# Folding the denominators of a sketched attention into its query sketch, in an attention and SwiGLU kernel on one core

## The chip, the core and the metric

The kernel runs on one core of a Trainium2 chip. A core has four engines that compute, each working through its own queue in order: TensorE (PE, matrix multiplies, with its weight loads shown as PEld), VectorE (DVE), ScalarE (ACT) and GpSimd (POOL). A fifth, SyncE (SP), issues transfers. The engines wait for each other through semaphores. Operands lie in SBUF, matmul results in the eight banks of PSUM, from which VectorE and ScalarE take them away. The metric is the device time of one execution in microseconds (us), lower is better.

## The reference

Two blocks follow each other. The first is an attention without a softmax over 4 batches, 4 heads, 1088 positions and 32 channels. Two 8x32 sketch matrices turn each query and key into two vectors of 8, whose outer product is a feature vector of 64:

```python
def phi(x):
    a = np.einsum('rd,bhsd->bhsr', S1, x)
    b = np.einsum('rd,bhsd->bhsr', S2, x)
    return np.einsum('bhsi,bhsj->bhsij', a, b).reshape(*x.shape[:-1], r * r)
q_p, k_p = (phi(q), phi(k))
kv = np.einsum('bhsf,bhsd->bhfd', k_p, v)
z = np.sum(k_p, axis=2)
num = np.einsum('bhsf,bhfd->bhsd', q_p, kv)
den = np.einsum('bhsf,bhf->bhs', q_p, z)[..., None] + 1e-06
```

Its result num / den, heads side by side, is a matrix x of 4352 tokens by 128. The second block is a SwiGLU layer with 1536 hidden channels: g = x @ w_gate, out = (g * sigmoid(g) * (x @ w_val)) @ w_out. Everything is float32.

## The kernel before

**Tiles.** A batch is cut into three blocks of 384, 384 and 320 tokens, so there are 12 blocks. The 1536 hidden channels are 12 chunks of 128. A unit is one block with one chunk. It makes the gate and the value products in PSUM, applies Silu on ScalarE and multiplies, which gives a tile of hidden values. `down` (L936) later multiplies that tile with a chunk of `w_out` and adds it up in the bank "acc". After 12 chunks `store` (L967) transposes the sum on VectorE and sends it out.

**Two kinds of unit.** A plain unit (`unit`, L903) has two float32 matmuls at L911 and one multiply on VectorE (L928). A cut unit (`cut_unit`, L868) replaces a float32 matmul by three in the type float32r, on operands that were split beforehand: weights into w1, wb and wd, tokens into x1, x0 and xd (`cut_weights` L835, `cut_tokens` L850). One (L877) makes a correction, two (L883, L884) add up the main part. ScalarE scales the correction (L889), VectorE joins the two (L892), and the multiply goes to GpSimd (L901). With both=False only the value product is made so and the gate product stays float32 (L879); with both=True both are.

**The order.** It is written out by hand (`manual_schedule`): the order in which Python emits instructions is the order in every engine's queue. Batch 0's attention comes first, in a form of its own, with the loading of the weights beside it. Then comes the head, a loop of 30 units of blocks 0 to 2 (z at L1140) in which downs start at z=17, and a flush of the remaining downs (L1160). The line then goes through the other nine blocks, y from 0 to 107 (L1177), twelve units to a block, each unit followed by a down of an earlier unit. In the line y below 38 is plain, 38 to 47 cuts the value product, 48 to 106 cuts both, and 107 is plain.

**The attention beside it.** The attentions of batches 1 to 3 are one Python generator (`attentions`, L563). The loops call it after a unit and it emits the next few instructions up to a `yield`; `group()` runs it up to a mark "pe". For each batch it transposes keys and queries on VectorE (`turns`), multiplies them with the sketch matrices on TensorE (`key_products` L332, `query_sketches` L320), makes key features on VectorE (L355), sums them on GpSimd (`feature_sums` L525), multiplies features with values and makes the key sums z (`values` L366, L678), and spreads both over the partitions with small transfers (`spread_out`). `query_step` (L706) then makes the denominators on VectorE: the first sketch of every query times z as products of 768 numbers a piece (L719), their sum (L726), times the second sketch (L735), summed, inverted. It scales the first sketch by the inverse, makes query features (L355) and transposes them (L750). `numerators` (L760) multiplies them on TensorE and copies the result to `xT`, the second block's input. For batch 1 numerators come in two parts, tokens of the first third before the line starts.

**PSUM.** Before y=36 units take banks in turn from three; from y=36 on (`oldest`) they take the one of seven that was touched longest ago, save those that are held.

Of the kernel before, what the change touches and what calls it, by code (L numbers as in the profile page):

```python
# [7 lines left out]
FP32 = mybir.dt.float32  # L8
# [11 lines left out]
def kernel(  # L20
# [280 lines left out]
    s12 = const.tile([P, 2 * H, 2, R], FP32, name="s12")  # L301
# [14 lines left out]
    def query_sketches(ps, c0, c1):  # L316

        for c in range(c0, c1):
            for a in range(4):
                nc.tensor.matmul(  # L320
                    ps[32 * a : 32 * a + 32, 64 * (c - c0) : 64 * (c - c0) + 64],
                    qT[:, 4 * c + a, :],
                    s12[:, a : a + H, :, :].rearrange("p h t r -> p (h t r)"),
                    start=True,
                    stop=True,
                )

    def key_products(ps, c0, c1):

        for c in range(c0, c1):  # L330
            for a in (0, 2):
                nc.tensor.matmul(  # L332
                    ps[32 * a : 32 * a + 64, 64 * (c - c0) : 64 * (c - c0) + 64],
                    kT[:, c, a : a + 2, :].rearrange("p a t -> p (a t)"),
                    s12[:, 0:H, :, :].rearrange("p h t r -> p (h t r)"),
                    start=True,
                    stop=True,
                )
# [182 lines left out]
    def feature_sums(phk):  # L521
# [4 lines left out]
        add(s[:], rows[:, 0:4, :], rows[:, 4:8, :])  # L526
        add(s[:, 0:2, :], s[:, 0:2, :], s[:, 2:4, :])
        add(s[:, 0, :], s[:, 0, :], s[:, 1, :])
        add(s[:, 0, :], s[:, 0, :], rows[:, 8, :])
        return s[:, 0, :]  # L530

    def turns(b):

        for c in kpieces:
# [3 lines left out]
            yield  # L538
        for x0, x1 in ((0, 4 * kpieces[0][1]), (4 * kpieces[0][1], 4 * NC)):
# [5 lines left out]
    def sketches(places):  # L545


        for products, i in ((key_products, 2), (query_sketches, 3)):
            for p in places:
                products(p[i], p[0], p[1])  # L550
        both = [
            apool.tile([P, 2, NC * H, R], FP32, tag=n, name=n, bufs=2) for n in ("kabs", "qab")
        ]

        def copy(t, c0, c1, ps):
            nc.scalar.copy(
                t[:, :, H * c0 : H * c1, :],
                ps[:, 0 : 64 * (c1 - c0)].rearrange("p (x t r) -> p t x r", t=2, r=R),
            )

        return both, [(copy, t, p[0], p[1], p[i]) for i, t in ((2, both[0]), (3, both[1])) for p in places]

    def attentions():  # L563
# [3 lines left out]

        yield from turns(1)
        hold("a", "b")
        kp, qp = wide("a"), wide("b")
        for ps, products in ((kp, key_products), (qp, query_sketches)):
            for i, c in enumerate(kpieces):
                products(ps[:, i, :], *c)
        ka = apool.tile([P, NC * H, R], FP32, tag="kas", name="kas")
        qab = apool.tile([P, 2, NC * H, R], FP32, tag="qab", name="qab", bufs=2)
        fac = None, qab  # L580
# [8 lines left out]
        for n, (i, c0, c1) in enumerate(((0, 0, 3), (0, 3, 5), (1, 5, 7), (1, 7, 9))):  # L589
# [3 lines left out]
            if n < 2:  # L593
                q0, q1 = kpieces[n]
                nc.scalar.copy(
                    qab[:, :, H * q0 : H * q1, :], sketch(qp, n).rearrange("p x t r -> p t x r")
                )
            if n == 1:
                release("b")
# [4 lines left out]
        zs = feature_sums(phk)  # L604
        for i, _ in enumerate(turns(2)):
            if i % 2:
                yield
        hold("a", "b")
        kvz = wide("a")
        values(kvz[:, 0, :], phk, zs)  # L610
        kq = wide("b")
        fac2, copies = sketches([
            (0, NC - 1, kq[:, 0], kq[:, 1]),
            (NC - 1, NC, kvz[:, 1, 0 : 2 * F], kvz[:, 1, 2 * F : 4 * F]),
        ])
        spread = spread_out(1, kvz[:, 0, :])
        for _ in range(4):
            yield
            run_copies(copies, 1)
        release("a", "b")  # L620
        step = query_step(1, fac, spread)
        yield from step(0, 3)
        numerators(1, spread, 0, 3)
        yield "first"
        yield from step(3, NC)
        phk = hbuf[:, NH - 6 :, :].rearrange("p s (n h i j) -> p (s n) h i j", h=1, i=R, j=R)
        phk = phk.rearrange("p (c h) o i j -> p c (h o) i j", h=H)
        yield from features(phk, fac2, ())
        zs = feature_sums(phk)
        yield from turns(3)  # L630
        yield "pe"
        numerators(1, spread, 3, NC)
        hold("a", "b")
        kv = bank()
        values(kv, phk, zs)
        kp, qp = wide("a"), wide("b")
        fac3, copies = sketches([(c0, c1, kp[:, i], qp[:, i]) for i, (c0, c1) in enumerate(kpieces)])
        spread = spread_out(2, kv)
        run_copies(copies, 2)
        yield  # L640
        run_copies(copies, 2)
        release("a", "b")
        yield
        yield from features(phk, fac3, ())
        zs = feature_sums(phk)
        yield from query_step(2, fac2, spread)(0, NC)
        yield "pe"
        numerators(2, spread, 0, NC)
        kv = bank()
        values(kv, phk, zs)  # L650
        spread = spread_out(3, kv)
        for _ in range(4):
            yield
        yield from query_step(3, fac3, spread)(0, NC)
        yield "pe"
        numerators(3, spread, 0, NC)
# [7 lines left out]
    def features(phk, fac, copies):  # L664
        kab = fac[0]
        for n, (c0, c1) in enumerate(((0, 3), (3, 5), (5, 7), (7, 9))):
            x = slice(H * c0, H * c1)
            key_features(phk, (kab[:, 0, x, :], kab[:, 1, x, :]), c0, c1)
            if copies:
                run_copies(copies, 1)  # L670
# [12 lines left out]
    def spread_out(b, kv):  # L683
# [3 lines left out]
        spread = apool.tile([P, H, 2, F], FP32, tag="spread", name="spread")  # L687
        nc.scalar.copy(
            spread[:, 0, 0, :].rearrange("p (j i) -> p j i", j=R),
            kv[:, F : 2 * F].rearrange("p (i j) -> p j i", j=R),  # L690
        )
        nc.vector.transpose(
            out=spread[:, 0, 1, :].rearrange("p (g d) -> p g d", g=2),
            in_=kv[:, 0:F].rearrange("p (g f) -> p g f", g=2),
        )
        for s in range(1, H):
            m = P - 32 * s
            nc.sync.dma_start(out=spread[0:m, s, :, :], in_=spread[P - m : P, 0, :, :])
            nc.sync.dma_start(out=spread[m:P, s, :, :], in_=spread[0 : P - m, 0, :, :])
# [6 lines left out]
    def query_step(b, fac, spread):  # L706
        zrep = spread[:, :, 0, :].rearrange("p h (j i) -> p h j i", j=R)
        qab = fac[1]
# [4 lines left out]

        def step(s0, s1):
            thirds = [c for c in fpieces if s0 <= c[0] < s1]
            for c0, c1 in thirds:
                n, x = c1 - c0, slice(H * c0, H * c1)
                f = qab[:, 0, x, :].rearrange("p (c h) i -> p c h i", h=H)
                nc.vector.tensor_tensor(  # L719
                    out=phq[:, c0:c1, :, :, :],  # L720
                    in0=zrep.unsqueeze(1).to_broadcast([P, n, H, R, R]),
                    in1=f.unsqueeze(3).to_broadcast([P, n, H, R, R]),
                    op=ALU.mult,
                )
                yield
                nc.vector.tensor_reduce(  # L726
                    out=dot[:, x, :],
                    in_=phq[:, c0:c1, :, :, :].rearrange("p c h j i -> p (c h) j i"),
                    axis=AX.X,
                    op=ALU.add,  # L730
                )
                yield
            x = slice(H * s0, H * s1)
            w = H * (s1 - s0)
            nc.vector.tensor_tensor(  # L735
                out=dot[:, x, :], in0=dot[:, x, :], in1=qab[:, 1, x, :], op=ALU.mult
            )
            nc.vector.tensor_reduce(out=den[:, x], in_=dot[:, x, :], axis=AX.X, op=ALU.add)
            nc.vector.tensor_scalar_add(den[:, x], den[:, x], 1e-6)
            nc.vector.reciprocal(den[:, x], den[:, x])  # L740
            nc.vector.tensor_tensor(
                out=qab[:, 0, x, :], in0=qab[:, 0, x, :],
                in1=den[:, x].unsqueeze(2).to_broadcast([P, w, R]), op=ALU.mult,
            )
            yield
            for c0, c1 in thirds:
                x = slice(H * c0, H * c1)
                key_features(phq, (qab[:, 0, x, :], qab[:, 1, x, :]), c0, c1)
                yield
                nc.vector.transpose(  # L750
                    out=phT[:, :, :, c0:c1, :].rearrange("p h g c t -> p c (h g) t"),
                    in_=phq[:, c0:c1, :, :, :].rearrange(
                        "p c h (g i) j -> p c (h g) (i j)", g=2
                    ),
                )
                yield

        return step

    def numerators(b, spread, s0, s1):  # L760
        kvr = spread[:, :, 1, :].rearrange("p h (g d) -> p h g d", g=2)
        phT = turned[b]
        num = wide("a"), wide("b")
        for g in range(2):
            for s in range(H):
                for a in range(4):
                    r = slice(32 * a, 32 * a + 32)
                    h = (a + s) % 4
                    n = min(s1, (NX - a + 3) // 4) - s0
# [3 lines left out]
                        phT[r, s, g, s0 : s0 + n, :],  # L773
# [472 lines left out]
```

## Time and profile before

| what | value |
|---|---|
| time, median of 3 runs | 292.65 us (292.53 to 292.82) |
| span of the profiled execution | 290.6 us |
| PE busy | 284.5 us (98%) |
| DVE busy | 200.7 us (69%) |
| ACT busy | 154.5 us (53%) |
| POOL busy | 130.1 us (45%) |
| units begin after the head, y=0 | 92.41 us |
| unit y=38, first cut of the value product | 169.06 us |
| unit y=48, first cut of both | 185.21 us |

Busy shares are averages over stages; the stages can be told apart by the source lines of the matmuls. Matmuls are pipelined and their recorded ends are modelled, so TensorE's pace is read from the starts of successive matmuls.

### The profile page before, as it was taken

To read this page: it belongs to the slowest core of one execution; us is meant where nothing else is said; L and a number is where in the kernel's file an instruction comes from. 1 tells how busy PE (TensorE), PEld (TensorE's weight loads), DVE (VectorE), ACT (ScalarE), POOL (GpSimd) and SP (SyncE) were. 2 spreads that over 40 slices of the span, in tenths; PEclk is the share of its full clock that TensorE was granted. 3 is DMA by queue.
4 is the path that set the end of the run, shared out by engine and by line. 5 is a ranking of instruction groups with operands and counts; after the bars stand their busy time and mean duration, and the time that the engine had idled before them with its cause. 6 is when DMAs were issued, how large, how long until landed. Compare 5 with 4: busy or idle time off the path is not lost.

```text
span 290.6 us, 6170 instructions
## 1 busy us (share of the span) xinstructions
PE 284.5 (98%) x2307; PEld 204.6 (70%) x2307; DVE 200.7 (69%) x400; ACT 154.5 (53%) x369; POOL 130.1 (45%) x144
## 2 busy tenths in 40 slices
PE   8899999999999999999999999999999999999995
PEld 7545566667666555755667677778788988888985
DVE  3997988875542997188893369997567675676651
ACT  3567565431301432353242365578688888888860
POOL 3215322138000308039741039676466676576650
PEclk9999999999999999999999999999999999999999
DMA  7564292315411100140010020001001010020101
GB/s 199 153 211 111 61 314 72 103 55 162 115 20 26 17 0 2 34 104 0 0 28 3 2 50 0 2 0 27 2 1 28 2 23 0 0 32 0 24 2 27
DMA packets 26142, 14.63 MB, mean 50 GB/s; under 512 B 18688, under 2 KB 24192, under 8 KB 26112
## 3 DMA queue, kind: packets, MB, share of 16 engines
q1 hardware_dynamic: 25456, 14.13, 19.1%
q8 instruction: 18, 0.29, 0.4%
q10 hardware_dynamic: 656, 0.10, 0.2%
q14 instruction: 12, 0.10, 0.1%
HBM read 11.41 MB, written 2.23 MB: 47 GB/s over the span
## 4 chain that ended last, share of the span: by engine, by line
PE 91%; DVE 3%; DMA 1%; issue 1%; ACT 1%; POOL 0%; SPq 0%; DVEq 0%
PE PS L911 32%; PE PS L942 28%; PE PS L877 7%; PE PS L883 7%; PE PS L884 7%; PE PS L879 2%; PE PS L770 2%; PE PS L332 2%; PE PS L366 2%; DMA kld<-in_k_dram 1%; PE PS L320 1%; DVE sum L892 1%; PE PS L957 1%; PE PS L475 1%; PE PS L423 1%
## 5 line engine op out<-in xcount | busy, mean ns | idle before, releaser
L942 PE MATMUL PS<-hbuf,wo 128*128 128x384 f32 (+2 forms) x288 | 104.7, 460 | 0.4 <-DVE o L971 0.4
L901 POOL TENSOR_TENSOR hbuf<-sg,sum 128x384 f32<-128x384 f32 (+1 forms) x69 | 69.8, 1015 | 53.6 <-ACT sg L896 31.4
L892 DVE SCALAR_TENSOR_TENSOR sum<-PS,sum 128x384 f32<-128x384 f32 (+1 forms) x128 | 62.7, 527 | 29.4 <-ACT sum L889 27.1
L917 ACT ACTIVATE sg<-PS 128x384 f32<-128x384 f32 (+1 forms) x75 | 35.4, 473 | 68.5 <-PE PS L911 66.1
L942 PEld LDWEIGHTS PS<-hbuf,wo 128*128 128x128 f32 x288 | 52.5, 189 | 17.6 <-issue 0.7
L911 PE MATMUL PS<-xT,wg 128*128 128x384 f32 (+1 forms) x150 | 59.1, 476 | 0.0
L911 PE MATMUL PS<-xT,wv 128*128 128x384 f32 (+1 forms) x150 | 58.3, 470 | 0.2 <-DVE wv L270 0.2
L889 ACT ACTIVATE sum<-PS 128x384 f32<-128x384 f32 (+1 forms) x128 | 53.3, 465 | 5.6 <-PE PS L877 5.2
L928 DVE TENSOR_TENSOR hbuf<-sg,PS 128x384 f32<-128x384 f32 (+1 forms) x69 | 36.1, 524 | 28.6 <-PE PS L911 26.8
L911 PEld LDWEIGHTS PS<-xT,wv 128*128 128x128 f32 x150 | 28.3, 190 | 17.9 <-DVE hbuf L928 0.9
L911 PEld LDWEIGHTS PS<-xT,wg 128*128 128x128 f32 x150 | 27.6, 190 | 18.2 <-issue 1.2
L896 ACT ACTIVATE sg<-sum 128x384 f32<-128x384 f32 (+1 forms) x59 | 29.7, 503 | 17.2 <-DVE sum L892 16.5
L877 PE MATMUL PS<-xd,gphq 128*128 128x384 f32 (+1 forms) x59 | 34.6, 587 | 0.0
L883 PE MATMUL PS<-x,w 128*128 128x384 f32 (+1 forms) x69 | 25.4, 368 | 0.0
L877 PE MATMUL PS<-xd,wd 128*128 128x384 f32 (+1 forms) x69 | 24.6, 357 | 0.0
L884 PE MATMUL PS<-x,wb 128*128 128x384 f32 (+1 forms) x69 | 22.6, 328 | 0.0
L883 PE MATMUL PS<-x,graw 128*128 128x384 f32 (+1 forms) x59 | 19.2, 325 | 0.0
L884 PE MATMUL PS<-x,graw 128*128 128x384 f32 (+1 forms) x59 | 19.1, 324 | 0.0
L877 PEld LDWEIGHTS PS<-xd,wd 128*128 128x128 f32 x69 | 13.1, 189 | 6.8
L838 POOL TENSOR_TENSOR low<-wv,w 128x384 f32<-128x384 f32 x4 | 4.7, 1176 | 25.4 <-ACT w L838 25.4
L877 PEld LDWEIGHTS PS<-xd,gphq 128*128 128x128 f32 x59 | 11.1, 189 | 6.4 <-issue 0.4
L525 POOL TENSOR_TENSOR zs<-hbuf 128x1024 f32<-128x1024 f32 x2 | 4.7, 2364 | 21.5 <-PE PS L911 11.6
(129 smaller groups left out, 340.7 us busy)
## 6 DMA issues: line engine op xcount, KB each, us to landing
kld<-in_k_dram SPq DMA_DIRECT2D x4, 544.0 KB, 4.2
vld<-in_v_dram SPq DMA_DIRECT2D x12, 144.0 KB, 4.8
qld<-in_q_dram SPq DMA_DIRECT2D x3, 544.0 KB, 3.8
raw<-in_moe_w_out_dram SPq DMA_DIRECT2D x4, 384.0 KB, 3.7
out_dram<-o SPq DMA_DIRECT2D x28, 48.0 KB, 1.9
raw<-in_moe_w_gate_dram SPq DMA_DIRECT2D x3, 384.0 KB, 3.2
raw<-in_moe_w_val_dram SPq DMA_DIRECT2D x3, 384.0 KB, 3.3
out_dram<-o SPq DMA_DIRECT2D x16, 40.0 KB, 1.7
```

The lines of the kernel that those rows point to most:

```text
L332: nc.tensor.matmul(ps[32 * a : 32 * a + 64, 64 * (c - c0) : 64 * (c - c0) + 64], kT[:, c, a : a + 2, :].rearrange("p a t -> p (a t)"), s12 ...
L877: nc.tensor.matmul(d, wd, xd, start=True, stop=True)
L883: nc.tensor.matmul(p, w1, x1, start=True, stop=False)
L884: nc.tensor.matmul(p, wb, x0, start=False, stop=True)
L889: nc.scalar.activation(s, d, AF.Copy, scale=-1.0 / BETA)
L892: nc.vector.scalar_tensor_tensor(out=s, in0=p, scalar=1.0 + 1.0 / BETA, in1=s, op0=ALU.mult, op1=ALU.add)
L896: nc.scalar.activation(sg, sums[0] if both else g, AF.Silu)
L901: nc.gpsimd.tensor_tensor(out=hj[:, 0:n], in0=sg, in1=sums[-1], op=ALU.mult)
L911: nc.tensor.matmul(o[:, 0:n], w[:, j, :], xT[:, t0 : t0 + n], start=True, stop=True)
L917: nc.scalar.activation(sg[:, 0:n], g[:, 0:n], AF.Silu)
L928: nc.vector.tensor_tensor(out=hj[:, 0:n], in0=sg[:, 0:n], in1=u[:, 0:n], op=ALU.mult)
L942: nc.tensor.matmul(acc[i][:, 0:n], wo[:, j, :], hidden[i, j][:, 0:n], start=(j == 0), stop=(j == NCH - 1),)
```

## The change

The denominators move from VectorE to TensorE. Since the denominator is a sum over i and j of a_i b_j z_ij, and a is the query times the first sketch, the kernel can fold z and the first sketch into a third sketch of 8x32 for each head and batch (`fold`: w_j = sum over i of z_ij S1_i). The query's matmul then gives three vectors of 8 instead of two, and the denominator is the product of the second and third, summed. The products with z and their sums go. The sketch matmul for queries widens from 64 to 96 columns, and it now has to wait for its batch's key sums.

The order is rewritten with it. Key and query turns are separate; batch 1's numerators come in one part; batches 2 and 3 are grouped at y=6, 8, 22, 24 and 40 instead of 12, 36 and 60. The operands of the value product are split during the head, so that all units of the line from y=0 cut the value product, and those from y=22 cut both, instead of from 38 and 48. The subtraction that makes `low` goes from GpSimd to VectorE. The first add of the feature sums, over 4 rows, becomes two of 2 rows, placed between other work. The oldest-bank rule and the hold of "acc" begin at y=0; a down follows its unit by five units instead of two from the line's start.

```diff
-                    ps[32 * a : 32 * a + 32, 64 * (c - c0) : 64 * (c - c0) + 64],
+                    ps[32 * a : 32 * a + 32, 96 * (c - c0) : 96 * (c - c0) + 96],
                     qT[:, 4 * c + a, :],
-                    s12[:, a : a + H, :, :].rearrange("p h t r -> p (h t r)"),
+                    s123[:, a : a + H, :, :].rearrange("p h t r -> p (h t r)"),
...
-        add(s[:], rows[:, 0:4, :], rows[:, 4:8, :])
-        add(s[:, 0:2, :], s[:, 0:2, :], s[:, 2:4, :])
+            lambda: add(s[:, 0:2, :], rows[:, 0:2, :], rows[:, 4:6, :]),
+            lambda: add(s[:, 2:4, :], rows[:, 2:4, :], rows[:, 6:8, :]),
+            lambda: add(s[:, 0:2, :], s[:, 0:2, :], s[:, 2:4, :]),
...
+    def fold(kv):
+        t = apool.tile([P, R, R], FP32, tag="fold", name="fold")
+        w = apool.tile([P, R], FP32, tag="w", name="w")
+        nc.vector.tensor_tensor(
+            out=t[:], in0=kv[:, F : 2 * F].rearrange("p (i j) -> p i j", j=R),
+            in1=sq[:, 0, :, :], op=ALU.mult,
+        )
+        nc.vector.tensor_reduce(
+            out=w[:], in_=t[:].rearrange("p i j -> p j i"), axis=AX.X, op=ALU.add
+        )
+        nc.vector.tensor_tensor(
+            out=s123[:, :, 2, :],
+            in0=w[:].unsqueeze(1).to_broadcast([P, 2 * H, R]),
+            in1=own2[:].unsqueeze(2).to_broadcast([P, 2 * H, R]),
+            op=ALU.mult,
+        )
...
-                nc.vector.tensor_tensor(
-                    out=phq[:, c0:c1, :, :, :],
-                    in0=zrep.unsqueeze(1).to_broadcast([P, n, H, R, R]),
-                    in1=f.unsqueeze(3).to_broadcast([P, n, H, R, R]),
-                    op=ALU.mult,
-                )
-                yield
-                nc.vector.tensor_reduce(
-                    out=dot[:, x, :],
-                    in_=phq[:, c0:c1, :, :, :].rearrange("p c h j i -> p (c h) j i"),
-                    axis=AX.X,
-                    op=ALU.add,
-                )
...
+        nc.vector.tensor_tensor(
+            out=dot[:], in0=qab[:, 1, :, :], in1=qab[:, 2, :, :], op=ALU.mult
+        )
+        nc.vector.tensor_reduce(out=den[:], in_=dot[:], axis=AX.X, op=ALU.add)
...
+        if z == 22:
+            lows = [fpool.tile([P, 3, P], FP32, tag="sgl", name="low", bufs=6)[:] for c in range(4)]
+            first, low, second, third = cut_weights(wv, [(nc.vector, low) for low in lows])
+        if z == 25:
+            take(low, 4)
...
-    PLAIN, VALUE = 3 * NCH + 2, 4 * NCH
+    GROUPS, GATES = (6, 8, 22, 24, 40), 22
...
-        if y in (NCH, 3 * NCH, 5 * NCH):
+        if y in GROUPS:
             group()
-        if y < PLAIN or y == END - 1:
+        if y == END - 1:
             unit(i, j)
         else:
-            cut_unit(i, j, both=y >= VALUE)
-        lag = LAG if y < PLAIN else min(5, END - y + 1)
+            cut_unit(i, j, both=y >= GATES)
         for _ in range(2):
-            if len(todo) > lag:
+            if len(todo) > min(5, END - y + 1):
                 down()
-        parts_of(2 if y in (0, 4, 6, 7, 8) else 1)
+        parts_of(y < GATES or y % 2 == 0)
+        if y == 0:
+            gate_rows = cut_weights(wg, [(nc.vector, low) for low in lows])
```

## The prediction

> **What bounds the kernel now.** First the page's busy shares and slices: TensorE is busy 98% of the span, at full clock, and no other engine comes near over the whole.
>
> ```profile
> PE 284.5 (98%) x2307; PEld 204.6 (70%) x2307; DVE 200.7 (69%) x400; ACT 154.5 (53%) x369; POOL 130.1 (45%) x144
> PE   8899999999999999999999999999999999999995
> DVE  3997988875542997188893369997567675676651
> ```
>
> The ends of matmuls are modelled, so I checked this in two views. TensorE's own waits come to about two microseconds in all, most at the start. Then TensorE in order of time, where a pace is the distance of equal starts:
>
> ```profile
> 160.54 0.70 PE L942 MATMUL PS<-hbuf,wo 128*128 128x320 f32 x2
> 162.15 0.70 PE L942 MATMUL PS<-hbuf,wo 128*128 128x320 f32 x2
> ...
> 174.33 0.63 PE L877 MATMUL PS<-xd,wd 128*128 128x384 f32 x1
> 176.15 0.63 PE L877 MATMUL PS<-xd,wd 128*128 128x384 f32 x1
> ...
> 186.91 0.63 PE L877 MATMUL PS<-xd,gphq 128*128 128x384 f32 x1
> 188.60 0.63 PE L877 MATMUL PS<-xd,gphq 128*128 128x384 f32 x1
> ```
>
> A plain unit of 320 tokens with its down takes 1.61 us (162.15 less 160.54). A unit of 384 takes 1.815 with the value product cut and 1.69 with both cut. A plain one of 384 is three float32 matmuls at 0.645 us (starts at 63.01, 63.65, 64.30), 1.935. These paces hold through each stage. So TensorE is a full queue from y=0 (92.4 us) to 280 us, and what it no longer has to do comes off the end, unless another engine makes it wait.
>
> The stretches show which engine that would be:
>
> ```profile
> 174.33:185.21 10.88, 10.88 (x44) 7.70 (x43) 10.42 (x18) 5.88 (x13) 8.88 (x8) 1.00 0.00 0
> 185.21:195.64 10.43, 9.98 (x49) 8.22 (x47) 10.28 (x18) 7.12 (x18) 7.76 (x7) 1.00 0.01 2
> 195.64:280.00 84.36, 84.36 (x487) 72.25 (x488) 55.59 (x115) 68.35 (x165) 53.73 (x58) 1.00 0.08 12
> ```
>
> Columns are the length, then PE, PEld, DVE, ACT, POOL. Where cut units run beside batch 3's attention, VectorE is busy 10.42 of 10.88 us and 10.28 of 10.43. There, at 195, TensorE loses its only visible time in the line, about 0.6 us. Without attention (last row) VectorE is at 66%.
>
> **What the Trainium skill says.** "FP8 and Floating Point Precision", TensorE Precision Notes: true FP32 makes four passes through the array. The trace agrees in ratio: a float32 matmul of 384 takes 0.645 us, one in float32r about 0.174 (186.03, 186.21, 186.38), 3.7 to 1. "GPSIMD Engine Reference", Performance versus the Vector engine: the elementwise sum of two tensors takes about twice as long on GpSimd. The trace agrees: the 128x384 multiply averages 1085 ns there (L901), 548 on VectorE (L928). "TensorE: Matmul & The Clock Gate", Back-to-back issue gap: 1 to 64 columns all cost a floor of some 25 ns. The query sketch's 72 matmul records, 64 columns each, start within 1.14 us (71.36 to 72.50), 16 ns a record in four column groups. That is under the floor, so the measurement decides, and the page can't promise that 96 columns cost no more.
>
> **Part by part.** *Cutting more products* (removed from TensorE). Newly cut are the value products of y=0 to 37 and the gate products of y=22 to 47. A cut at 384 saves 0.12 us (1.935 to 1.815 to 1.69). At 320, plain is 1.612 and both cut 1.412 (starts 220.44, 221.85), so 0.10 each. Values: 26 x 0.12 + 12 x 0.10 = 4.3 us. Gates: 14 x 0.12 + 12 x 0.10 = 2.9 us. Together -7.2 us.
>
> *Numerators of batch 1 in one part*: before 0.89 and 1.18 us (88.73 to 89.62, 114.51 to 115.69), in one part 1.5 (162.78 to 164.28): -0.6 us.
>
> *Sketch of 96 columns*, three bursts. No row shows that width. From below nothing, as the issue may bind; from above 1.14 x 96/64, 0.57 more each. I take 0.4: +1.2 us, ends 0 and 1.7.
>
> *VectorE loses the products with z*: 3 products and 3 sums a batch at 1158 and 946 ns, 6.3 us a batch, 19 in all. It gains the fold: multiply, sum and spread of 64 to 576 numbers. The smallest like rows (a 128x64 transpose, a 128x12 sum) take 0.25 us each, so about 0.9 us a batch with the waits, 0.75 to 1.5. It gains 8 subtractions at 0.55, 4.4 us. The cut itself moves the multiply from VectorE (548) to GpSimd and brings a join (551), which is even for values, but adds 0.5 us a unit for gates.
>
> *The head's end.* Before, VectorE needed one third of batch 1's query step before the first numerators; now it needs all. After the last head unit's multiply come a product (0.62), a sum (0.45), two short ones (0.4), a scaling (0.62), then three times 1.02 and 0.97: about 8.2 us with gaps. Meanwhile TensorE has 12 downs of 384 and one of 320, 12 x 0.645 + 0.54 = 8.3 us. The multiply starts 0.3 us after the unit's matmul and takes 0.5, so numerators come about 0.7 us late, 0 to 1.5. Behind them 11 downs of 0.54 us (5.9) hide the copy to xT, the split of the tokens and one feature product, about 3.7 us. The four value subtractions fall into a stretch where VectorE is at 50% (16.2 of 32.4 us from 60 to 92.4). The split add costs GpSimd some 0.3 us before batch 1's key sums, which today end just as TensorE arrives (end 69.85, start 69.93): +0.3.
>
> *Batch 2's key sums at y=6.* The first six units have no down, so TensorE passes them in 6 x 1.17 = 7.0 us. Then come a down 0.65 and the key values 1.02: it asks for the sums 8.7 us after y=0. GpSimd has the adds between the first multiplies: the first add waits for features that end about y=0, the second stands behind the multiply of unit 0, which waits for its join on VectorE behind a transpose (about 2 us after y=0). From there 4 multiplies at 1.085 and adds of 1.35, 1.35, 0.73 and 1.0 end about 8.8 us later, so 10.0 to 10.8 us after y=0. TensorE waits 1.3 us, bounds 0.5 and 2.5. Everything in TensorE's queue stands behind that wait.
>
> *y=24 to 37, both cut beside batch 3's query step.* VectorE: joins 24 x 0.448 (21.5 over 48) and 4 x 0.515, 12.8; denominators 2.2; features and transposes 6.0; a store and a token split 1.1: 22.1 us. TensorE: five units at 1.52, seven at 1.41, two at 1.585: 20.7 us. VectorE is 1.4 us short; the banks let it fall about one unit behind, but the 2.2 us of denominators come as one lump. I take +1.0, 0 to 2. Waits for banks where sketches and numerators take four at once (y=8, 22, 24): +0.3, 0 to 0.8. The stall of 0.6 at 195 goes.
>
> Edits taken at nothing: more room for sg and fewer hidden slots (17 for five waiting units), the spreading transfers, now half as wide, and the copies on GpSimd at the start, which fall where it waited 4.4 us for VectorE anyway.
>
> Sum: -7.2 - 0.6 - 0.6 = -8.4; +1.2 + 0.7 + 0.3 + 1.3 + 1.0 + 0.3 = +4.8. Net -3.6: 292.65 becomes 289.0 us.
>
> **Rivals.** (A) The waits hide: lag and banks take up the head's end, the key sums and y=24 to 37. Then -8.4 + 1.2 + 0.3 leaves 285.7 us. For it speaks that VectorE ran at 98% at 185 to 195 and cost TensorE only 0.6; against it, that the key sums at y=6 and the numerators stand in TensorE's own queue. (B) VectorE or GpSimd becomes the bound over y=0 to 40: costs at their upper ends, 1.7 + 1.5 + 0.5 + 2.5 + 2.0 + 0.8 = 9.0 against 8.4 gained, no change, 292.6 to 293.2 us. For it speaks GpSimd's load: over y=0 to 21 it has 22 multiplies (23.9), adds for two batches (12), four weight parts (4) and two token parts (2.1), 42 us, while TensorE passes in about 40 (6 x 1.17, 16 x 1.815, bursts of 4); five units of lag hide most of that. (C) Slower: the same, and the waits feed each other, a late join holding banks so that units stop at every attention step, 0.15 us more on 40 units: 6 us above my sum, 295 us. Against it speaks that VectorE has 19 us less of attention.
>
> **How the numbers follow.** Forecast 0.62, A 0.18, B 0.13, C 0.07. The range takes in most of A's side and part of B: 286.3 to 291.9. Faster by over 0.2% (below 292.07): forecast, A and a part of B, 0.86. Same 0.05, slower 0.09.
>
> **What would show it.** Right: units at y=0 to 21 paced at 1.81 us, from y=24 at 1.41 to 1.52, from y=36 at 1.6 to 1.7; a wait of TensorE on GpSimd's sums once, near y=6; numerators of batch 1 waiting on VectorE's transpose under 1.5 us; VectorE near 100% at y=24 to 37. The sketch burst's length settles 96 columns. Wrong: bank waits repeated through the line, or a burst over 1.8 us.

## The result, and the profile after

The changed kernel takes 295.05 us (median of 4 runs, 294.86 to 295.23); the kernel before took 292.59 us on the same chip (292.43 to 292.82). The ratio is 1.0083 with a 95% interval of 1.0066 to 1.0101: slower by about 2.46 us, where 289.0 had been forecast with a range that ends at 291.9. One thing is needed to compare the traces below: in two of them the first 16 us, which no experiment edits, took 1.3 us longer than in the others (the first value product starts at 17.30 and 17.50 us, elsewhere at 15.6 to 16.2), and what follows is that much later.

TensorE has less to do and is worse fed. On the page of the changed kernel:

```profile
PE 280.7 (96%) x2307; PEld 212.2 (72%) x2307; DVE 209.1 (71%) x422; ACT 182.2 (62%) x432; POOL 164.3 (56%) x183
PE   7899999998989989989998999999999999999995
```

Its busy time fell from 284.5 to 280.7 us while the span grew from 290.6 to 293.0. GpSimd (POOL) rose from 130.1 to 164.3 us. VectorE rose too, 200.7 to 209.1, although some 19 us of denominator work had left it. The slices that read 8 for TensorE all end by 161 us.

TensorE's own waits in the changed kernel (engine, what waited and for what; total us, times, longest):

```profile
PE PS L941 <- DVE o L970: 2.0, 2, 1.0
PE PS L336 <- DVE kT L309: 1.9, 2, 1.3
PE PS L701 <- POOL zs L529: 1.4, 1, 1.4
PE PS L763 <- DVE phT L745: 1.3, 1, 1.3
```

One of the four had been forecast at about this size as a wait on GpSimd (the key sums, L701), one at half its size (numerators, L763), two not at all: key transposes in the head (L336), and downs that wait until `store` has emptied the bank "acc" (L941). Of the 1.9 us at L336, 0.67 lie at 6 us and cost nothing: what follows begins no later than before (12.79 us, 12.92 before). TensorE in order of time shows where each lies (start, length, instruction, and in brackets the idle time just before it):

```profile
71.14 0.69 PE L336 MATMUL PS<-s,kT 128*64 128x64 f32 x16 [1.26 <-DVE kT L309]
...
73.67 1.69 PE L324 MATMUL PS<-s,qT 128*32 128x96 f32 x72
75.30 0.81 PE L910 MATMUL PS<-xT,wg 128*128 128x320 f32 x2
...
87.96 1.57 PE L763 MATMUL PS<-phT,spread 32*32 32x288 f32 x64 [1.32 <-DVE phT L745]
...
95.24 0.58 PE L876 MATMUL PS<-xd,wd 128*128 128x384 f32 x1
...
105.84 0.32 PE L701 MATMUL PS<-zs,ones 128*32 128x64 f32 x8 [1.40 <-POOL zs L529]
...
114.37 0.63 PE L876 MATMUL PS<-xd,wd 128*128 128x384 f32 x1
116.18 0.63 PE L876 MATMUL PS<-xd,wd 128*128 128x384 f32 x1
...
131.50 0.88 PE L941 MATMUL PS<-hbuf,wo 128*128 128x384 f32 x2 [1.01 <-DVE o L970]
...
157.75 0.78 PE L941 MATMUL PS<-hbuf,wo 128*128 128x320 f32 x2 [0.95 <-DVE o L970]
...
173.21 0.70 PE L941 MATMUL PS<-hbuf,wo 128*128 128x320 f32 x2
...
177.62 0.70 PE L941 MATMUL PS<-hbuf,wo 128*128 128x320 f32 x2
```

The line now begins at 95.24 us, 2.83 later than the 92.41 of before. Two waits of 1.26 and 1.32 us stand ahead of it; the matmuls of the head come out even (one sketch burst of 1.63 in place of two of 1.14, numerators 0.6 longer). In the line a unit is paced at 1.81 us (116.18 less 114.37), as forecast. To find what the line lost, I took the distance between successive downs and subtracted what the matmuls between them cost where nothing is waited for:

| place in the line | lost, us |
|---|---|
| key sums of batch 2, y=6 | 1.82 |
| down behind the store, y=17 (131.50) | 1.16 |
| down behind the store, y=29 (157.75) | 1.49 |
| y near 35 | 0.44 |
| numerators and unit at y=40, 173.21 to 177.62 in place of 3.08 | 1.33 |
| small ones at sketches and numerators (0.19, 0.29, 0.20, 0.11) | 0.8 |
| ends of three later blocks, 0.22 each | 0.7 |
| sum | 7.7 |

The same reckoning gives 1.9 us for the line before (0.62, 0.67, 0.37, 0.20). Work changed by -7.2 us (cuts), -0.6 (numerators of batch 1) and +1.5 (three bursts 0.49 longer), -6.3 in all. So -6.3 + 2.83 + (7.7 - 1.9) = +2.33 us, against +2.4 between the two spans.

Why VectorE comes late shows in its own order of time in the changed kernel:

```profile
65.71 4.75 DVE L847 TENSOR_TENSOR low<-wv,w 128x384 f32<-128x384 f32 x4
70.39 0.70 DVE L309 STREAM_TRANSPOSE kT<-kld 128x512 f32<-128x512 f32 x1
...
118.42 1.42 DVE L359 TENSOR_TENSOR hbuf<-kab 128x768 f32<-128x768 f32 x1
...
120.23 2.42 DVE L359 TENSOR_TENSOR hbuf<-kab 128x512 f32<-128x512 f32 x2
...
131.29 1.93 DVE L359 TENSOR_TENSOR phq<-qab 128x768 f32<-128x768 f32 x1
133.13 0.55 DVE L891 SCALAR_TENSOR_TENSOR sum<-PS,sum 128x384 f32<-128x384 f32 x1
133.60 0.96 DVE L745 STREAM_TRANSPOSE phT<-phq 128x768 f32<-128x768 f32 x1
```

The four subtractions that make `low` take 4.75 us, 1.19 each, where 0.55 had been assumed, and the key transpose that TensorE waits for at 71.14 stands directly behind them. Feature products of one form take 1.42 and 1.93 us at different times, while joins (0.55) and transposes (0.96) keep their length. GpSimd over the same time:

```profile
118.02 1.00 POOL L847 TENSOR_TENSOR gphq<-graw 128x384 fp32r<-128x384 f32 x1
118.98 1.72 POOL L900 TENSOR_TENSOR hbuf<-sg,sum 128x384 f32<-128x384 f32 x1
120.66 1.45 POOL L847 TENSOR_TENSOR gphq<-graw 128x384 fp32r<-128x384 f32 x1
```

It works without a gap, and its instructions lengthen as well: 1.00 us where one starts ahead of VectorE's feature (118.02 against 118.42), 1.72 and 1.45 where a feature is already under way. This is what the Trainium skill describes in "SBUF — State Buffer", Who interferes with whom: a VectorE instruction with two inputs in SBUF contends with a GpSimd instruction that reads SBUF; one with at most one such input does not, outside of some fast modes. Features made from `kab` or `qab`, `low` and the denominator's product have two. A join has one, its other input being in PSUM, and a transpose has one. The prediction never drew on that page.

### The profile page after: what moved, and what is told of

It is laid out like the page before. It is cut to its first block, busy times and chain, and to the rows that moved or that the text cites. A ratio compares the mean times of both kernels' runs of the same rounds, so it can differ in the third digit from the quotient of the medians.

```text
span 293.0 us, 6383 instructions
## 1 busy us (share of the span) xinstructions
PE 280.7 (96%) x2307; PEld 212.2 (72%) x2307; DVE 209.1 (71%) x422; ACT 182.2 (62%) x432; POOL 164.3 (56%) x183
## 4 chain that ended last, share of the span: by engine, by line
PE 77%; DVE 10%; POOL 6%; issue 3%; ACT 2%; DMA 1%; SPq 0%; DVEq 0%; POOLq 0%
PE PS L941 23%; PE PS L910 15%; PE PS L876 10%; PE PS L882 9%; PE PS L883 9%; POOL hbuf L900 2%; PE PS L878 2%; POOL zs L529 2%; PE PS L324 2%; PE PS L763 2%; DVE sum L891 2%; PE PS L336 2%; DMA kld<-in_k_dram 1%; POOL gphq L847 1%; DVE low L847 1%
## 5 line engine op out<-in xcount | busy, mean ns | idle before, releaser
L900 POOL TENSOR_TENSOR hbuf<-sg,sum 128x384 f32<-128x384 f32 (+1 forms) x107 | 108.0, 1011 | 58.5 <-ACT sg L895 51.6
L891 DVE SCALAR_TENSOR_TENSOR sum<-PS,sum 128x384 f32<-128x384 f32 (+1 forms) x192 | 93.9, 526 | 50.8 <-ACT sum L888 43.6
L941 PE MATMUL PS<-hbuf,wo 128*128 128x384 f32 (+2 forms) x288 | 104.9, 461 | 2.1 <-DVE o L970 2.0
L888 ACT ACTIVATE sum<-PS 128x384 f32<-128x384 f32 (+1 forms) x192 | 80.6, 466 | 14.5 <-PE PS L876 13.8
L941 PEld LDWEIGHTS PS<-hbuf,wo 128*128 128x128 f32 x288 | 51.3, 189 | 12.1 <-POOL x L858 2.1
L916 ACT ACTIVATE sg<-PS 128x384 f32<-128x384 f32 (+1 forms) x37 | 17.5, 475 | 23.1 <-PE PS L910 21.5
L910 PE MATMUL PS<-xT,wg 128*128 128x384 f32 (+1 forms) x74 | 29.5, 480 | 0.0
L910 PE MATMUL PS<-xT,wv 128*128 128x384 f32 (+1 forms) x74 | 28.8, 471 | 0.2 <-DVE wv L270 0.2
L882 PE MATMUL PS<-x,graw 128*128 128x384 f32 (+1 forms) x85 | 27.7, 326 | 0.0
L883 PE MATMUL PS<-x,graw 128*128 128x384 f32 (+1 forms) x85 | 27.6, 325 | 0.0
L927 DVE TENSOR_TENSOR hbuf<-sg,PS 128x384 f32<-128x384 f32 (+1 forms) x31 | 16.1, 522 | 9.9 <-PE PS L910 9.5
L882 PEld LDWEIGHTS PS<-x,w 128*128 128x128 f32 x107 | 20.1, 188 | 3.8 <-ACT sum L888 0.4
L883 PEld LDWEIGHTS PS<-x,wb 128*128 128x128 f32 x107 | 20.1, 188 | 2.9
```

What stands on the lines that cost most here:

```text
L882: nc.tensor.matmul(p, w1, x1, start=True, stop=False)
L883: nc.tensor.matmul(p, wb, x0, start=False, stop=True)
L888: nc.scalar.activation(s, d, AF.Copy, scale=-1.0 / BETA)
L891: nc.vector.scalar_tensor_tensor(out=s, in0=p, scalar=1.0 + 1.0 / BETA, in1=s, op0=ALU.mult, op1=ALU.add)
L900: nc.gpsimd.tensor_tensor(out=hj[:, 0:n], in0=sg, in1=sums[-1], op=ALU.mult)
L910: nc.tensor.matmul(o[:, 0:n], w[:, j, :], xT[:, t0 : t0 + n], start=True, stop=True)
```

## The experiments

All runs were made beside the kernel before, which read 292.5 to 292.7 us each time; each ratio is to that kernel. The question throughout was whether the waits come from VectorE and GpSimd slowing each other, or from the order of the queues and their load, which would be the same with every instruction at its undisturbed length. An edit is against the changed kernel unless another is named.

**The four `low` subtractions two head units later.**

```diff
-        if z == 25:
+        if z == 27:
             take(low, 4)
```

> Only the place of the four value subtractions (low) in VectorE's queue is changed: after head unit z=27 instead of before the second key transpose at z=25. Theory 1 (VectorE and GpSimd slow each other when both read and write SBUF alone, and the queue's order passes the delay on): at the new place GpSimd is idle, so the four take about 0.55 us each instead of 1.19, the wait of TensorE of 1.26 us on the key transpose goes, and y=0 begins 1.0 to 1.4 us earlier; 293.6 to 294.1 us. Theory 2 (VectorE has too much work for TensorE's faster pace, wherever it stands): they take 1.19 us again, the delay moves behind them to the numerators, 295.0 us.

293.6 us, ratio 1.0037 (1.0024 to 1.0049). VectorE in this run, at a time when GpSimd is idle for 5.75 us:

```profile
72.26 1.96 DVE L847 TENSOR_TENSOR low<-wv,w 128x384 f32<-128x384 f32 x4
```

1.96 us for the four instead of 4.75 (0.55 each, started 0.47 apart), the key transpose is no longer held up, y=0 begins at 93.89 (1.35 earlier) and the time falls by 1.45 us.

**The same, with GpSimd made busy beside it.** Against the run above; four subtractions of the same size are added on GpSimd, whose result nothing uses.

```diff
         if z == 27:
-            take(low, 4)
+            beside_low = fpool.tile([P, 3, P], FP32, tag="sgl", name="beside", bufs=6)[:]
+            for c in range(4):
+                take(low, 1)
+                nc.gpsimd.tensor_tensor(
+                    out=beside_low, in0=wv[:, 0:3, :], in1=wg[:, 0:3, :], op=ALU.subtract
+                )
```

> As the first of this batch, with four subtractions of the same size added on GpSimd beside the four on VectorE; nothing reads their result. Theory 1: the four on VectorE go back to about 1.1 to 1.2 us each and those on GpSimd take more than 1.0 each; VectorE idles 3 us there, so the time rises by only 0 to 0.8 us over the first of this batch. Theory 2 (the subtraction is slow by itself): 1.19 us in both.

294.7 us, ratio 1.0073 (1.0051 to 1.0095). VectorE, then GpSimd, in this run:

```profile
73.53 3.83 DVE L847 TENSOR_TENSOR low<-wv,w 128x384 f32<-128x384 f32 x4
```

```profile
71.85 4.63 POOL L1167 TENSOR_TENSOR beside<-wv,wg 128x384 f32<-128x384 f32 x4
```

Position and order on VectorE are the same in both runs; only GpSimd differs. VectorE's four go from 1.96 to 3.83 us. Singly they take 0.81, 1.36 and 1.35 us while GpSimd works, and the fourth, which GpSimd no longer meets, 0.55 (1.1 to 1.2 had been expected for each). Of GpSimd's four the two that start ahead of VectorE's take 1.00 each, the other two 1.21 and 1.19. That VectorE and GpSimd slow each other in such instructions is shown by this pair. The page named above, under "SBUF: two separate sides", speaks of an exclusive lock: whoever starts first has the ports for the whole instruction, and the other is blocked. One of each in turn would take 1.47 us here (1.00 and 0.47). VectorE's second and third start 1.28 us apart (74.26 and 75.54), so in these records the two overlap a little.

The longer wait then appears at the numerators, 1.9 us instead of 1.3. This 0.56 us is all that the added work costs in this trace, inside the 0 to 0.8 expected. The rest of its distance to the run above is the late start: the first value product comes at 17.30 us, 1.26 later than there, and the line is no longer (192.4 us in both). The four executions fall into two pairs about as far apart, 293.8 and 294.1, 295.3 and 295.4.

**The cuts undone, the folded denominators kept.** Value products plain up to y=37 and gate products up to y=47, as before.

```diff
-    GROUPS, GATES = (6, 8, 22, 24, 40), 22
+    GROUPS, GATES = (6, 8, 22, 24, 40), 48
...
-        if y == END - 1:
+        if y == END - 1 or y < 3 * NCH + 2:
...
-        parts_of(y < GATES or y % 2 == 0)
+        parts_of(y < 22 or y % 2 == 0)
```

> The denominators, the groups and the order of the changed kernel, but values and gates cut only where the kernel before cut them (38 and 48); token and weight parts are still made early. Theory 1: the cuts still bring TensorE about 7.2 us and cost some 3 us of waits in the line, so without them it is 298 to 300 us. Theory 2: the cuts are what overloads VectorE and GpSimd, so without them the waits in the line (about 6 us) go and the time is 294 to 296 us.

297.04 us, ratio 1.0148 (1.013 to 1.0165), between what was expected. The earlier cuts are therefore worth 2.0 us in the changed kernel and not 7.2; the line's lost time in this run is 2.3 us in place of 7.7, which accounts for the rest. The new attention form with its order and with the parts still made early costs 4.4 us against the kernel before: longer sketch bursts, the head's waits (1.3 at the key transposes and 1.3 at the numerators again), and the `low` subtractions remain in it.

**Gate products cut from y=42 instead of 22.**

```diff
-    GROUPS, GATES = (6, 8, 22, 24, 40), 22
+    GROUPS, GATES = (6, 8, 22, 24, 40), 42
...
-        parts_of(y < GATES or y % 2 == 0)
+        parts_of(y < 22 or y % 2 == 0)
```

> Gates cut from y=42 instead of y=22, after the last attention. TensorE loses 20 cuts, 2.2 us. Theory 1: only the waits at y=29 to 40 (1.3 at the store, 0.4, and 1.0 at the numerators at y=40) go, 2.7 us: 294.3 to 294.9 us. Theory 2: VectorE's load falls by 0.5 us a unit and more goes with it: 292.5 to 293.5 us.

294.49 us, ratio 1.0074 (1.0062 to 1.0087), 0.56 less than with 22. Twenty units give up 8 x 0.12 + 12 x 0.10 = 2.2 us of savings; the losses at y=29 (1.49) and y=35 (0.44) go and that at y=40 falls from 1.33 to 0.42, 2.8 us. So cutting gates beside batch 3's attention costs more than it saves. In the changed kernel the store at y=29 stood behind a join that itself waited 0.88 us for ScalarE, which scales twice per unit there and had a token split before it; features beside it took 0.95, so this wait is one of load, not of the two engines slowing each other.

**A second bank for sums of downs.** Against the first experiment.

```diff
-            acc[i] = bank("g1" if i == 1 else "acc")
+            acc[i] = bank("g1" if i == 1 else "g2" if i > 3 and i % 2 == 0 else "acc")
...
-    hold("acc")
+    hold("acc", "g2")
```

> On top of the late value subtractions: a second bank for the sums of the down products, so that a block's first down needn't wait until VectorE has transposed the block before it; units have six banks left instead of seven. Theory 1: the two waits of TensorE on the store at y=17 and y=29 (1.2 and 1.3 us) go, 2 to 2.5 us, and at most 0.5 comes back as bank waits: 291.3 to 292.0 us. Theory 2 (VectorE is simply behind there): the same time is lost a unit later as bank waits, 293.3 to 294 us.

294.04 us, ratio 1.0057 (1.004 to 1.0074): not better than the first experiment's 293.6. The waits for the store are gone and come back one step on, as waits for banks: 1.73 us at the numerators of y=22, then 0.45, 0.38, 0.37, 0.65, 0.81, and 1.35 at y=40. From y=0 to the last down the line takes 192.6 us (93.83 to 286.45) against 192.2 without the edit (93.89 to 286.10). This fits a VectorE that is late whichever instruction of TensorE's queue meets it first. But the second sum takes a bank from the units, six in place of seven, and no run separates that from the lateness.

**More downs ahead of the numerators.** Against the first experiment.

```diff
     while todo:
-        for _ in range(min(3, len(todo))):
+        for _ in range(min(6 if len(todo) == 14 else 3, len(todo))):
             down()
```

> On top of the late value subtractions: three more downs of 0.54 us stand ahead of batch 1's numerators, eight behind. Theory 1: the wait of 1.33 us for VectorE's last transpose goes, and the eight downs (4.3 us) still hide the copy and the split (3.4 us): 292.2 to 292.6 us. Theory 2: the copy and split come out instead, 293.2 to 293.7 us.

295.79 us, ratio 1.0115 (1.0099 to 1.0131): every expectation missed. The line starts 1.64 us earlier, at 92.25, but a store now stands ahead of the last key features in VectorE's queue, so GpSimd gets them later while TensorE asks for the sums earlier. TensorE waits 3.6 us for them. What comes after that wait was the surprise; TensorE in this run:

```profile
105.04 0.32 PE L701 MATMUL PS<-zs,ones 128*32 128x64 f32 x8 [3.59 <-POOL zs L529]
...
107.07 1.48 PE L878 MATMUL PS<-xT,wg 128*128 128x384 f32 x2
107.78 1.09 PE L882 MATMUL PS<-x,w 128*128 128x384 f32 x1
...
110.19 0.81 PE L878 MATMUL PS<-xT,wg 128*128 128x384 f32 x2
110.53 0.63 PE L882 MATMUL PS<-x,w 128*128 128x384 f32 x1
```

The same two matmuls take 0.71 us from start to start right after the wait and 0.34 three microseconds later: the clock was halved. The granted clock is 0.50 from 106.33 to 109.74 us and 1.00 on both sides of it.

**Gate-weight subtractions later.** Against the first experiment.

```diff
-            if y >= (0, 2, 7, 9)[n]:
+            if y >= (0, 7, 11, 13)[n]:
                 take(row, 1)
```

> On top of the late value subtractions: the four gate subtractions on VectorE begin at y=7 instead of y=2, the two rows after them at y=11 and 13. Theory 1: GpSimd's adds and multiplies of y=0 to 4 no longer stand beside them and the wait of TensorE on the key sums falls from 1.4 to 0.2 to 0.8 us; later VectorE is more crowded, so 292.7 to 293.4 us. Theory 2 (the adds are late because of their place behind the multiplies): no change, 293.5 us.

295.38 us, ratio 1.0097 (1.0066 to 1.0129), the time is off again. The key sums' loss falls from 1.84 to 0.60, as meant. One of GpSimd's adds, first in the first experiment and then in this run:

```profile
99.78 1.60 POOL L529 TENSOR_TENSOR zs<-zs 128x512 f32<-128x512 f32 x1
```

```profile
99.07 1.30 POOL L529 TENSOR_TENSOR zs<-zs 128x512 f32<-128x512 f32 x1
```

GpSimd's queue is the same in both and without a gap from the second add on. Its next four instructions took 1.33, 1.60, 1.33 and 1.03 us beside VectorE's subtractions and take 1.02, 1.30, 1.02 and 0.75 without them. So 1.2 of the 1.8 us lost at y=6 come from the two engines slowing each other, with no order changed on GpSimd.

The subtractions and GpSimd's share of them now lie beside batch 2's query step, TensorE waits 2.2 us at y=17 for the store, and its clock is 0.50 from 130.00 to 133.41 us. Three of the six executions granted a mean clock of 0.994, as this trace; two of the others took 294.3 us without a fall, some 1.4 less, and were still slower than the first experiment. A gain at one place was lost twice at another.

**The last three edits together.**

> All three edits of this batch together. Theory 1: the gains add up, 289.5 to 291.0 us, faster than the kernel before. Theory 2: VectorE is the bound up to y=40 and the time comes to 292.5 to 293.5 us whatever is moved.

295.98 us, ratio 1.0104 (1.0083 to 1.0125). In the trace the sums' wait is 2.3 us and the clock stays full; this is one of two executions of 294.5 us, while the other four, 295.9 to 296.4, granted a mean of 0.994. The edits that start TensorE earlier make it meet the sums sooner than these are done; they don't add.

**Batch 2's sums on GpSimd without multiplies between them.** Against the first experiment. The four adds are emitted together, before key transposes of batch 3, instead of one after each unit.

```diff
-        yield from beside(turn_keys(3), sums)
         while sums:
             sums.pop(0)()
-            yield
+        yield from beside(turn_keys(3), sums)
```

> On top of the late value subtractions: batch 2's four adds of the key sums stand together ahead of the first multiplies on GpSimd, not between them. Theory 1 (places in the queues, slowed by both engines reading SBUF): the wait of 1.84 us at y=6 goes and nothing else moves, 291.8 to 292.3 us. Theory 2 (VectorE or GpSimd bound up to y=40): the multiplies come later by as much, waits show up at the downs of y=6 to 17, 293.3 to 294 us.

292.03 us, ratio 0.9982 (0.9972 to 0.9992), 1.6 us less than the first experiment, and the loss at y=6 is gone but for 0.2. Order alone can thus take that wait away, whatever had lengthened it: the first units' multiplies stood between the adds in GpSimd's queue, while the hidden tiles that they make are not asked for until later.

**The head's end as well.** Against the run above: the numerators get three more downs ahead of them, the tokens of batch 1 are split in one go, and two steps of attention follow each group of downs, which puts the key features ahead of the store.

```diff
-        for _ in range(min(3, len(todo))):
+        for _ in range(min(6 if len(todo) == 14 else 3, len(todo))):
             down()
-        if begun[0]:
-            x_steps = x_steps or cut_tokens(HEAD, nc.vector)
-            next(x_steps, None)
-        parts_of(1)
+        if begun[0] and not x_steps:
+            x_steps = cut_tokens(HEAD, nc.vector)
+            run(x_steps)
+        parts_of(2 if begun[0] else 1)
```

> On top of the adds together: three more downs ahead of batch 1's numerators, and the tokens' split and the key features of batch 2 ahead of the store in VectorE's queue, which last time held up the last feature product. Theory 1: the wait of 1.33 us at the numerators goes too, 290.6 to 291.2 us, faster than the kernel before. Theory 2: given back at y=6 or y=17, 292.5 to 294 us.

291.57 us, ratio 0.9971 (0.9959 to 0.9983). The numerators start without a wait, yet only 0.46 of their 1.3 us arrives at the end. The two traces show where the rest went. This one starts 0.26 us later (first value product at 16.23 against 15.97). From there to y=0 it is 1.41 shorter (76.47 against 77.88), so the whole wait is gained. The line is then 0.83 longer (92.70 to 284.07 against 93.85 to 284.39): at 100.66 a down waits for a multiply that GpSimd hasn't reached, and 0.73 us go with it.

**Gate weights prepared later and gates cut from 42.** Against the run above.

```diff
-    GROUPS, GATES = (6, 8, 22, 24, 40), 22
+    GROUPS, GATES = (6, 8, 22, 24, 40), 42
...
-        parts_of(y < GATES or y % 2 == 0)
-        if y == 0:
+        parts_of(y < 22 or y % 2 == 0)
+        if y == 22:
             gate_rows = cut_weights(wg, [(nc.vector, low) for low in lows])
...
-            if y >= (0, 2, 7, 9)[n]:
+            if y >= (28, 34, 36, 38)[n]:
```

> On top of the head's edit: gates cut from y=42, and the weights of the gate product split between y=28 and 41, away from the adds and from batch 2's query step. 20 gate cuts less cost 2.2 us; the waits at y=17, 29, 35 and 40 (1.2, 1.5, 0.45 and 1.0 us) should go. Theory 1: 288.5 to 290.5 us. Theory 2: 292 us or more.

290.49 us, ratio 0.9927 (0.9905 to 0.9948): faster than both kernels, by 2.2 us than the one before, which took 292.7 beside it, and by 4.6 us than the changed one. The trace is of the longest of its six executions, 292.02 us, with the late start (17.50 us). The down behind the store at y=17 and one of the features ahead of that store, in the run above:

```profile
115.09 1.42 DVE L359 TENSOR_TENSOR hbuf<-kab 128x768 f32<-128x768 f32 x1
...
128.17 0.88 PE L940 MATMUL PS<-hbuf,wo 128*128 128x384 f32 x2 [1.00 <-DVE o L969]
```

and in this run:

```profile
115.97 0.95 DVE L359 TENSOR_TENSOR hbuf<-kab 128x768 f32<-128x768 f32 x1
...
128.31 0.88 PE L940 MATMUL PS<-hbuf,wo 128*128 128x384 f32 x2 [0.21 <-DVE o L969]
```

For the store at y=17 these two runs are a test that changes nothing in VectorE's queue. From y=8 to that store it has the same instructions in the same order in both, since its own four subtractions for the gate weights stood earlier, at 97 to 102 us. What has gone is four subtractions on GpSimd (1.00, 1.45, 1.45 and 1.00 us, 114.7 to 123.7) and four roundings on ScalarE, for which nothing in VectorE's queue waited. VectorE's feature products ahead of the store fall from 6.15 to 4.67 us, and the time lost at that down from 1.16 to 0.38.

The store at y=29 no longer holds TensorE up, as with the gate cuts from 42 alone; a wait of 0.4 us at a later store (216.30) came with those cuts too (218.67 there), and 0.5 us for the gate weights that GpSimd now prepares late (176.49) are new.

**The multiply of y=8 to 21 back on VectorE.** Against the first experiment.

```diff
-        nc.gpsimd.tensor_tensor(out=hj[:, 0:n], in0=sg, in1=sums[-1], op=ALU.mult)
+        mul = nc.vector if by_vector[0] else nc.gpsimd
+        mul.tensor_tensor(out=hj[:, 0:n], in0=sg, in1=sums[-1], op=ALU.mult)
...
+            by_vector[0] = 8 <= y < 22
             cut_unit(i, j, both=y >= GATES)
```

> On top of the late value subtractions alone: the multiply of units y=8 to 21 on VectorE instead of GpSimd, which has then only the adds and weight parts there. Theory 1: VectorE's feature products there fall from 1.2 to 1.9 us back to about 0.95, but it gets 14 multiplies of 0.55 us, 7.7 us, so its load up to y=22 rises and the time is 294 to 297 us. If instead the features stay at 1.2 us and more, GpSimd's multiplies are not what slows them.

302.34 us, ratio 1.0325 (1.0304 to 1.0346). VectorE in this run:

```profile
119.64 0.56 DVE L903 TENSOR_TENSOR hbuf<-sg,sum 128x384 f32<-128x384 f32 x1
120.11 0.95 DVE L359 TENSOR_TENSOR hbuf<-kab 128x768 f32<-128x768 f32 x1
...
122.11 1.29 DVE L359 TENSOR_TENSOR hbuf<-kab 128x512 f32<-128x512 f32 x2
...
123.97 1.28 DVE L903 TENSOR_TENSOR hbuf<-sg,sum 128x384 f32<-128x384 f32 x1
```

The features that took 1.42 and 2.42 us are back at 0.95 and 1.29 with GpSimd idle, which settles whose doing their length was. The multiply itself takes 0.56, and 1.28 where a GpSimd sum has started ahead of it (123.57). The time is far above the 294 to 297 expected: 14 multiplies more than VectorE can carry, waits of 2.8 and 2.5 us, and a clock of 0.50 from 130.84 to 141.08.

## Why the prediction was wrong

**Cuts, -7.2.** Right. The paces named as signs are there: 1.81 at y=0 to 21, 1.52 and 1.41 after y=24, about 1.6 to 1.7 from y=36.

**Sketch of 96 columns, +1.2.** 0.49 a burst measured, +1.5, inside the bounds given. **Batch 1's numerators in one part, -0.6.** Right. **The split add, +0.3.** 0.16 measured: 1.18 us from the key values to the key sums (67.64, 68.82), 1.02 before.

**The head.** "The four value subtractions fall into a stretch where VectorE is at 50%" is the first step that failed. It priced eight subtractions at 0.55 and let a mean hide them. A mean over 32 us says nothing of what stands behind four instructions in the queue, and the price was that of the instruction undisturbed (0.55 in the first experiment). The four for the values took 1.19 each and cost 1.26 us; moving them alone gave 1.45 us back. The numerators were forecast to wait 0.7 us (0 to 1.5) and waited 1.3: right in kind, mis-sized.

**The key sums at y=6, +1.3.** Lost 1.82, inside 0.5 to 2.5, and that is in part luck: with the order described and VectorE's subtractions out of the way it was 0.60, so 1.2 came from a cause that the prediction didn't have. It was costed and not asked about further; the run with the adds together shows it was avoidable.

**"*y=24 to 37* ... I take +1.0, 0 to 2", and bank waits +0.3.** This is the step that failed most. y=8 to 21 was given no cost at all, and there VectorE was busy 23.95 of 24.63 us. All attention durations came from a kernel in which GpSimd had few multiplies beside batch 2's attention; the change moves the multiply of every value unit to GpSimd, and puts the gate weights' subtractions between them. Features with two SBUF inputs then run up to twice as long, and so do GpSimd's multiplies. The prediction called the move of the multiply "even for values", 548 ns against a join of 551. Even on VectorE's count it was; on its durations it wasn't. Of the 1.16 us at y=17, 0.8 go with GpSimd's four gate-weight subtractions, the multiplies staying. The trace of before held a sign of this, in the product with z (L719) of one batch:

```profile
129.65 2.07 DVE L719 TENSOR_TENSOR phq<-spread,qab 128x768 f32<-128x768 f32 x1
...
133.52 0.95 DVE L719 TENSOR_TENSOR phq<-spread,qab 128x768 f32<-128x768 f32 x1
```

At 129.65 GpSimd was already at an add of the key sums (128.54 to 130.90). The prediction took the mean, 1158 ns. And the accumulating bank wasn't treated as a resource: one bank, emptied by VectorE once a block, is where lateness meets TensorE's queue. Against 1.3 us taken for both terms the line lost 1.16 + 1.49 + 0.44 + 1.33 and the small ones.

**The stall of 0.6 at 195** went, and others took its place. It hadn't been the only one: by the reckoning above the line before lost 1.9 us.

**Rivals.** C, slower at 295, had the time right with a chance of 0.07, and its argument half right: a late VectorE meets TensorE at stores and numerators, in a few single waits of over a microsecond and not in 0.15 us on each of 40 units. What was said against it, "VectorE has 19 us less of attention", was cancelled: VectorE's busy time rose by 8.4 us.

**What is shown, and what stays open.** The wait at the key transposes and two losses of the line come in the main from the two engines slowing each other: the four `low` subtractions take 4.75 and 3.83 us beside GpSimd and 1.96 without it, and 1.2 of 1.8 us at y=6 and 0.8 of 1.2 at y=17 go when the other engine's subtractions are taken away from beside it, the late engine's own queue kept in its order. Those from y=29 on are of load, since they go or shrink with the gate cuts. The same order that makes the engines meet decides where it hurts: other places in the queues took the waits at the key transposes and at y=6 away. Open is how much of the 1.3 us at the numerators of the head is due to which, and whether the remaining 0.4 at y=17 is load alone.

## What to carry to other kernels

An instruction's duration belongs to its neighbours too: before work is moved to GpSimd, look for VectorE instructions with two SBUF inputs that will run beside it, and price both at up to double. When a bound engine is freed of work, walk its queue for each point where it takes a result from another engine (sums, transposes, an emptied accumulator) and ask what stands ahead of that result in the other engine's queue; shares of busy time over a stretch hide exactly this. And when a wait turns up, first try another order of the same instructions: here that, with a later start of the gate cuts, gave 4.6 us, where a second bank for the sums, taken from the units, gave nothing.

## What the runs showed of the hardware

- 128x384 float32 subtractions, one on VectorE and one on GpSimd, all inputs in SBUF: 0.55 and 1.00 us when alone, up to 1.36 and 1.21 together. Instructions of VectorE with PSUM as one input (0.55) and its transposes (0.96) kept their length beside the same GpSimd work.
- TensorE's clock was halved for 3.41 us after waits of 3.6 and 2.2 us in a queue otherwise full, and for 10.24 us around waits of 2.8 and 2.5 us. The Trainium skill, "TensorE: Matmul & The Clock Gate", What's actually happening, puts the idle time at about one window of 3.4 us that doesn't start with the kernel; the 3.6 us agrees, the 2.2 us is under it. In the 3.41 us just ahead of each of the three falls TensorE was busy for 1.29, 1.25 and 1.02 us, so it needn't be idle for a whole window. A trace with a wait of 2.3 us had no fall: in steps of 3.41 us from where its clock became full, that wait lies across two, with 2.54 and 1.94 us busy. That fits windows at fixed places, and that executions of one kernel came with a fall and without, 1.4 us apart.
- A burst of 72 records of 96 columns takes 1.63 us, 22.6 ns a record, where one of 64 columns takes 16: time followed the columns nearly in full (1.43 to 1), so the smaller burst had no floor that would have hidden the wider one.
